# Cosine-weighted attention with a mixture of adapters: narrower moving operands for two kinds of matmul, and a mask applied before the sigmoid

## The chip, the cores and the metric

The kernel runs on one core of one Trainium2 chip. The metric is the device time of one execution in microseconds (us). Three executions of the kernel before took 107.39, 108.11 and 108.67 us; their median is 108.11 us. The profile was taken of one further execution.

A core has five engines with queues of their own: TensorE (PE in the profile; PEld is its weight load), VectorE (DVE), ScalarE (ACT), GpSimd (POOL) and SyncE (SP). All of them feed the same 16 DMA engines.

## The reference, cut to what matters

```python
# q, k, v: (8, 8, 576, 64);  w_gate: (512, 8);  A: (8, 512, 16);  B: (8, 16, 512)
theta = pi / 2 * arange(S) / S
phi(x) = concat([relu(x) * cos(theta), relu(x) * sin(theta)], -1)     # 128 features
q_p, k_p = phi(q), phi(k)
kv  = einsum('bhsf,bhsd->bhfd', k_p, v)
z   = sum(k_p, axis=2)
num = einsum('bhsf,bhfd->bhsd', q_p, kv)
den = einsum('bhsf,bhf->bhs', q_p, z)[..., None] + 1e-6
x   = (num / den), heads side by side: (4608, 512)
...
logits = x @ w_gate
the two largest of 8 logits get softmax weights w, the others none
out = x + sum over the two experts e of  w_e * ((x @ A[e]) @ B[e])
```

For two kept logits the softmax weight of one is a sigmoid of the difference: with s the sum of the two largest, the weight of logit l is sigmoid(2l - s).

## The kernel before, in words

There are eight batches of eight heads with 576 tokens of 64 numbers. The output is made in 36 tiles of 128 rows (two token positions of 64 rows each), numbered n.

Inputs are loaded on POOL's DMA queue (`load_k`, `load_v`, `load_q`, lines 124 to 143), which turns float32 into bfloat16 on the way; only k of batch 0 goes by SP's queue as float32 (`k0f`). There are five buffers each for k, q and v, so batches 5, 6 and 7 reuse buffers of earlier ones; v of batch 5 goes where v of batch 0 was. For batches 1 to 7 the 576 tokens lie on 128 partitions as nine token slots: one half of the partitions has five, the other four (`NJ` = 5, `long_half`). Token slots s = 0 to 3 thus fill 128 partitions, and the fifth, s = 4, only 64 (`half_of`). Batch 0 has another layout with nine slots of 64 partitions.

For each batch and slot, `scale_k1` (line 236) makes the cosine and sine halves of the key features on ScalarE, VectorE or POOL; a relu before POOL's version is `relu_k` on VectorE (line 264). `kv(b, s)` (line 277) then issues eight matmuls, one per head, into two PSUM banks `cd`: the key features are the stationary operand, and the moving operand (`v_rhs`, line 269) is two pieces of 64 columns: v of this head and slot, and 64 columns of ones at the end of the v tile (line 177). So each matmul has 128 columns, of which the first 64 give kv and each of the others gives z. `kv_out` (line 291) copies 65 of them per head.

For each tile n: `transp_q` (Q, line 320) turns q and scales it by a diagonal matrix, `evac_q` (E) applies the relu, `numden` (N, line 364) multiplies by the 65 columns of kv and z, `normalise` (R, lines 375 to 386) divides, `transp_x` and `evac_x` (X and C, lines 394 and 401) turn the result. `logits` (L, line 421) multiplies it by `AW`: 128 columns of all experts' A, then 16 columns of which eight hold the gate weights and eight are zeros (`ZW` = 144). `AW` is filled by two loads (lines 205 and 207) with each expert's columns apart, so the moving operand is nine pieces of 16.

Tiles are gated in groups of three (eleven groups, then one of two tiles and one of one). `gate_a` (A, lines 430 to 438, VectorE) finds the two largest logits, their sum `nm`, the mask of kept logits and `tg` = 2l - nm. `gate_sig` (S, line 447, ScalarE) writes the sigmoid beside the products in PSUM. `gate_b` (B, lines 454 and 456, VectorE) multiplies sigmoid and mask to `em`, and the expert products by `em` to `zg`. Then `transp_z` (Z), `evac_z` (Y), `delta` (O, lines 488 and 489) and `evac_o` (V, lines 502 and 505) follow; for ten tiles `add_x` (P, line 496) adds x on POOL. `store` (T, line 515) writes the 256 KB of a tile by SP's queue.

The order of the work is written out by hand: the words of `ORDER` (lines 31 to 66) are carried out one after the other, under a schedule that keeps each engine to the order in which its instructions are issued. Stores are held back: the load before the last pair (q of batch 7) is followed by a tiny transfer on SP's queue that reads what it brought (`first_loads`, line 562), and every store stands behind that transfer. Before `ORDER`, lines 518 to 544 do the start: tables, 24 warm-up matmuls (line 524), batch 0's keys, and the loads of the next batches and of the weights.

Of the kernel before, what the change touches and what calls it, by code (L numbers as in the profile page):

```python
# [11 lines left out]
ALU = mybir.AluOpType  # L12
# [19 lines left out]
R0 Q1.0 Q1.1 E1.0.a E1.1.d X0 Q2.0 K1.0.0.a K1.2.0.d N1 E2.0.a Q2.1 R1 H E2.1.a Q3.0 C0.a  # L32
K1.4.1.d N2 K1.3.1.d K1.0.1.a Q3.1 R2 H K1.1.0.a X1 H H C1.a K1.2.1.d H E3.0.d E3.1.a M1.2
K1.1.1.a M1.0 K1.3.0.d K1.4.0.d N3 X2 R3 M1.1 M1.3 M1.4 C2.d Q4.0 W1 Q4.1 H E4.0.a E4.1.d H Q5.0
N4 E5.0.a Q5.1 R4 H E5.1.a X3 Q6.0 Q6.1 C3.d E6.0.a H K2.3.1.d N5 E6.1.a U2.0.2 X4 H R5 K2.4.0.a
L0 Q7.0 K2.4.1.a Q7.1 K2.3.0.d N6 G2.0 C4.d E7.0.a L1 R6 L2 E7.1.a X5 Q8.0 C5.a Q8.1 G2.1 A0 N7
E8.0.a X6 R7 M2.4 S0 C6.a Dq.3 M2.3 E8.1.a M2.0 B0 N8 M2.1 U2.2.3 F8 G2.2 L3 R8 L4 L5 Z0 A1 Q9.0
Y0.a Q9.1 Dk.4 M2.2 E9.0.d S1 E9.1.a X7 B1 W2 Q10.0 Q10.1 C7.d E10.0.a N9 O0 X8 R9 E10.1.a Z1 L6
K3.2.0.a L7 O1 U3.0.2 C8.a.1 N10 V0.d G3.0 Q11.0 Q11.1 V1.a R10 L8 E11.0.a O2 E11.1.a G3.1 O3 X9
V2.a V3.d Q12.0 Q12.1 K3.2.1.a A2 N11 Dv.4 M3.0 K3.4.1.d M3.1 S2 K3.3.0.a C9.d M3.2 K3.4.0.d  # L40
E12.0.a R11 X10 Dq.4 M3.4 E12.1.a K3.3.1.a Dk.5 Q13.0 B2 Q13.1 N12 E13.0.a C10.d M3.3 F12
E13.1.a X11 R12 Z2 Dv.5 L9 W3 Q14.0 C11.d.2 Q14.1 N13 E14.0.a O4 U4.0.2 F13 E14.1.a U4.2.3 O5
G4.0 R13 X12 V4.a Q15.0 Q15.1 C12.a V5.d N14 E15.0.a L10 G4.1 K4.4.0.d O6 E15.1.a L11 R14 X13 O7
C13.a Dk.6 Q16.0 V6.d V7.a Q16.1 N15 E16.0.a K4.4.1.d X14 A3 M4.0 F15 E16.1.a G4.2 M4.1 R15 S3
C14.a Q17.0 Q17.1 B3 E17.0.a N16 Dq.5 X15 E17.1.a M4.2 R16 C15.a L12 Dk.7 O8 K4.3.1.a L13 V8.d
L14 N17 K4.3.0.a Z3 A4 Q18.0 F17 Q18.1 Y3.a R17 M4.4 Dq.6 E18.0.a M4.3 S4 E18.1.a U5.0.2 X16 B4
W4 G5.0 Q19.0 Q19.1 C16.d E19.0.a N18 L15 K5.4.1.d E19.1.a X17 R18 O9 G5.1 C17.a Q20.0 Q20.1
E20.0.a L16 V9.d O10 E20.1.a L17 Dv.6 K5.4.0.d N19 V10.d Z4 F19 Q21.0 Y4.a Q21.1 R19 K5.3.1.a
M5.4 M5.1 E21.1.a E21.0.d X18 K5.3.0.a U5.2.3 N20 A5 M5.0 G5.2 F20 C18.a O11 R20 O12 S5 X19
V12.a M5.3 Dq.7 V11.d M5.2 C19.a B5 N21 Dv.7 W5 Q22.0 R21 Q22.1 E22.0.a X20 O13 E22.1.a K6.2.1.d  # L50
Q23.0 C20.a K6.3.1.d N22 U6.0.2 E23.0.a Q23.1 K6.3.0.d G6.0 X21 K6.2.0.d F22 Z5 E23.1.a L18 R22
V13.a Q24.0 Q24.1 E24.0.a C21.d.5 L19 L20 E24.1.a N23 U7.0.2 O14 A6 X22 F23 G7.0 V14.a Q25.0 R23
Q25.1 S6 E25.0.a O15 O16 E25.1.a G6.1 B6 N24 C22.a Q26.0 R24 Q26.1 E26.0.a L21 Z6 P14 X23
E26.1.a L22 U7.2.3 C23.d.6 N25 V15.a Q27.0 V16.a G7.1 R25 Q27.1 X24 K6.4.0.a L23 M6.1 A7 E27.0.a
M6.2 P16 E27.1.a C24.d N26 O17 K6.4.1.a K7.3.0.d M6.0 V17.d M6.3 F26 S7 R26 M6.4 Q28.0 W6 B7
Q28.1 X25 E28.0.a N27 K7.3.1.d O18 C25.d E28.1.a O19 L24 R27 V18.a Z7 T0 X26 Q29.0 P18 C26.a.7
Q29.1 T1 V19.d N28 L25 E29.0.a T2 R28 O20 P15 X27 E29.1.a L26 T3 O21 C27.a Q30.0 V20.d T4 Q30.1
G7.2 V21.a X28 A8 N29 E30.0.a T5 M7.1 R29 E30.1.a M7.0 T6 C28.a O22 M7.3 T7 S8 V22.d K7.4.0.a
N30 X29 T8 B8 K7.4.1.a M7.2 T9 Q31 F30 C29.d M7.4 E31.0.d E31.1.a T10 L27 W7 L28 R30 T11 Z8 L29
Y8.a T12 Q32.0 A9 N31 E32.0.a T13 Q32.1 R31 S9 X30 E32.1.a O23 T14 O24 V23.a Q33 C30.d T15 V24.a  # L60
N32 B9 T16 E33.0.a X31 P24 O25 R32 L30 C31.a T17 O26 E33.1.a V26.d Z9 T18 P21 X32 V25.a N33
# [8 lines left out]
def kernel(ctx, tc, q, k, v, w_gate, A, Bw, out):  # L70
# [7 lines left out]
    ZW = ER + R  # L78
# [17 lines left out]
    VN = H * NJ * D  # L96
# [13 lines left out]
    v_b = [persist.tile([128, VN + D], BF16, name=f"v{b}") for b in range(5)]  # L110
    v_b += v_b[:3]
# [26 lines left out]
    def load_v(b):  # L138
        if b == 0:
            x = v_b[b][:, 0:G * NS * D].rearrange("p (g x) -> p g x", g=G)  # L140
# [35 lines left out]
    for t in v_b[:5]:  # L176
        nc.vector.memset(t[:, VN:], 1.0)
    ones = persist.tile([128, 128], BF16, name="ones")
# [21 lines left out]
    AW = persist.tile([128, E + 1, DCH, R], BF16, name="AW")  # L200
    nc.vector.memset(AW[:, E], 0.0)  # L201
    Ball = persist.tile([128, DM], BF16, name="Ball")

    def load_weights():
        nc.gpsimd.dma_start(out=AW[:, 0:E].rearrange("p e c r -> p e (c r)"),
                            in_=A.rearrange("e (p c) r -> p e (c r)", c=DCH))
# [6 lines left out]
    g_t, u_t, den_t = {}, {}, {}  # L213
# [55 lines left out]
    def v_rhs(b, at, pr):  # L269
        base = v_b[b][pr, at * D:(at + 1) * D]  # L270
        p, (step, n) = base.ap[0], base.ap[-1]
        return bass.AP(base.tensor, base.offset, [p, [(VN - at * D) * step, 2], [step, n]])
# [4 lines left out]
    def kv(b, s):  # L277
        first, last = kv_n[b] == 0, kv_n[b] == kv_all[b] - 1
        kv_n[b] += 1
        for g in range(G):  # L280
            for par in range(2):
                if b == 0:
                    pr = (lo, hi)[par]
                    lhsT, rhs = kp_t[b][pr, s, g], v_rhs(b, g * NS + s, pr)
# [3 lines left out]
                nc.tensor.matmul(out=kvz[par][:, g], lhsT=lhsT, rhs=rhs,  # L288
                                 start=(first and g == 0), stop=(last and g == G - 1))
# [119 lines left out]
    def logits(n):  # L409
        g = group_of[n]  # L410
        i = n - groups[g][0]
        if i == 0:
# [5 lines left out]
            u_t[g] = t[:, 3 * ZW:3 * ZW + 3 * E].rearrange("p (i e) -> p i e", e=E)  # L418
        xT = xT_t.pop(n)
        for c in range(DCH):  # L420
            nc.tensor.matmul(out=za_t[g][:, i, :], lhsT=xT[:, c, :], rhs=AW[:, :, c, :],  # L421
# [3 lines left out]
    def gate_a(g):  # L425
# [3 lines left out]
        for i in range(n):  # L429
# [6 lines left out]
                                in1=m8[:, 0:n, 1].to_broadcast([128, n, 8]), op=ALU.is_ge)  # L436
# [4 lines left out]
        g_t[g] = (t, mask)  # L441

    def gate_sig(g):
        n = len(groups[g])
        t, mask = g_t[g]
        u = u_t.pop(g)
        nc.scalar.activation(u[:, 0:n], t[:, 0:n], AF.Sigmoid)
        g_t[g] = (u, mask)

    def gate_b(g):  # L450
        n = len(groups[g])
        u, mask = g_t[g]
        em = p_g.tile([128, 3, 8], FP32, name="em")
        nc.vector.tensor_tensor(out=em[:, 0:n], in0=u[:, 0:n], in1=mask[:, 0:n], op=ALU.mult)
# [154 lines left out]
```

## Time and profile before

| what | value |
|---|---|
| median of three runs | 108.11 us (107.39 to 108.67) |
| profiled execution, its own time | 107.45 us |
| its span, from first to last instruction | 105.7 us |
| TensorE busy | 94.8 us (90%) |
| VectorE, ScalarE, POOL busy | 87.5, 84.5, 63.1 us |
| POOL's DMA queue (loads) | 13.84 MB, 88.5% of the 16 engines' time |
| SP's DMA queue (first load and stores) | 10.62 MB, 27.0% |

In rows that give groups of instructions, the columns are line, engine, operation, what is written from what is read, shapes and count, then busy time in us and mean ns of one, then idle time before them and what ended it. In rows by time, the first two numbers are the start and the length of a merged run of like instructions, and `x16` is their number. In sums by window there is, behind the window and its length, one busy time for each engine with the number of instructions in brackets, then the granted clock of TensorE, the DMA share and GB/s. Where a window is restricted to one line of the kernel, only the engines that have it are given. In the chain of waits, the numbers are start, length and what the end of the program hung on.

### The profile page before, as it was taken

Reading aid. Unit: us, or ns where it says so; the run is one execution under the profiler, and the core shown is the slowest. Engines: PE = TensorE matmul, PEld = TensorE weight load, DVE = VectorE, ACT = ScalarE, POOL = GpSimd, SP = SyncE. Lnnn points to the kernel's source line nnn. Section 1 sums busy time; section 2 is a strip of 40 time slices with the busy share of each in tenths; the row PEclk is TensorE's granted clock in tenths of the full one; section 3 lists DMA queues with packets and bytes.
Section 4 is the critical chain, followed back from the end, with each engine's and each line's share of the span. In section 5 each row is a group of like instructions: output and inputs, shape, how many; then the busy total and the mean of one; then the engine's idle time right before and its main releaser. Section 6 shows DMA issues by size and latency. Waiting matters only on the chain.

```text
span 105.7 us, 4237 instructions
## 1 busy us (share of the span) xinstructions
PE 94.8 (90%) x1696; PEld 72.6 (69%) x1696; DVE 87.5 (83%) x305; ACT 84.5 (80%) x184; POOL 63.1 (60%) x94
## 2 busy tenths in 40 slices
PE   2999879999999999999899999998999999998700
PEld 1335765876898878877787887867888986775200
DVE  5489469859989989989999999999999998799510
ACT  4359459649975999898999999999699979997800
POOL 5995342254979099899939575699329102984000
PEclk9999999999999999999999999999999999999995
DMA  2999999999999999999999999999799899898991
GB/s 31 372 230 206 200 201 200 204 190 187 205 205 198 202 204 204 193 208 201 198 196 203 206 205 203 198 210 199 99 344 367 333 380 346 325 356 311 385 383 69
DMA packets 26995, 24.72 MB, mean 234 GB/s; under 512 B 2784, under 2 KB 21856, under 8 KB 26976
## 3 DMA queue, kind: packets, MB, share of 16 engines
q0 software_dynamic: 21248, 13.84, 88.5%
q1 hardware_dynamic: 5728, 10.62, 27.0%
q8 instruction: 13, 0.21, 0.7%
q14 instruction: 6, 0.05, 0.1%
HBM read 28.85 MB, written 9.44 MB: 362 GB/s over the span
## 4 chain that ended last, share of the span: by engine, by line
PE 66%; DMA 12%; DVE 11%; ACT 3%; issue 3%; DVEq 0%; ACTq 0%
PE cd L288 15%; PE qd L320 12%; DMA AW<-in_moe_w_gate_dram 12%; PE za L421 8%; PE nd L364 8%; PE wu L524 8%; PE xz L394 7%; PE cd L489 4%; DVE xt L386 3%; PE xz L469 2%; DVE osb L505 2%; PE cd L488 1%; PE dx L489 1%; DVE xT L401 1%; DVE rden L379 1%
## 5 line engine op out<-in xcount | busy, mean ns | idle before, releaser
L336 ACT ACTIVATE qpT<-qd 128x512 bf16<-128x512 f32 x65 | 37.1, 608 | 3.1 <-PE qd L320 2.1
L257 POOL TENSOR_SCALAR kp<-k,tab_kv 128x512 bf16<-128x512 bf16 x32 | 22.0, 697 | 9.5 <-DVE k L267 4.4
L386 DVE TENSOR_TENSOR xt<-nd,rden 128x512 bf16<-128x512 f32 x36 | 24.9, 692 | 2.1
L320 PE MATMUL qd<-diag,q 128*64 128x128 bf16 x544 | 22.8, 223 | 0.1
L288 PE MATMUL cd<-v,kp 128*128 128x128 bf16 (+1 forms) x352 | 21.8, 218 | 0.0
L320 PEld LDWEIGHTS <-q 128*64 128x64 bf16 x544 | 16.7, 110 | 4.6 <-issue 2.0
L288 PEld LDWEIGHTS <-kp 128*128 128x128 bf16 (+1 forms) x352 | 18.2, 96 | 2.2 <-DVE kp L254 0.4
L496 POOL TENSOR_TENSOR osb<-osb,xt 128x512 f32<-128x512 f32 x10 | 11.4, 1159 | 11.1 <-ACT osb L502 11.1
L364 PE MATMUL nd<-kvsb,qpT 128*128 128x65 bf16 (+1 forms) x320 | 15.3, 194 | 1.4 <-DVE xt L386 0.9
L394 PE MATMUL xz<-ident,xt 128*128 128x128 bf16 x144 | 14.1, 221 | 1.3 <-DVE xT L401 0.5
L364 PEld LDWEIGHTS <-qpT 128*128 128x128 bf16 (+1 forms) x320 | 12.1, 100 | 3.4 <-issue 1.0
L421 PE MATMUL za<-AW,xT 128*128 128x144 bf16 x140 | 13.3, 227 | 0.2 <-DMA AW<-in_moe_w_gate_dram 0.2
L394 PEld LDWEIGHTS <-xt 128*128 128x128 bf16 x144 | 10.4, 114 | 3.9 <-DVE xt L386 1.4
L252 ACT ACTIVATE kp<-k,tab_kv 128x512 bf16<-128x512 bf16 (+1 forms) x18 | 12.6, 724 | 0.4 <-DMA k<-in_k_dram 0.3
L502 ACT COPY osb<-cd 128x512 f32<-128x512 f32 x21 | 12.2, 608 | 0.4 <-PE cd L489 0.3
L401 ACT COPY xT<-xz 128x512 bf16<-128x512 bf16 (+1 forms) x19 | 12.3, 648 | 0.2 <-PE xz L394 0.2
L127 POOL DMA_DIRECT2D v<-in_v_dram x14 | 9.7, 701 | 2.7 <-DMA v<-in_v_dram 2.5
L421 PEld LDWEIGHTS <-xT 128*128 128x128 bf16 x144 | 9.7, 98 | 2.3 <-issue 0.7
L127 POOL DMA_DIRECT2D k<-in_k_dram x14 | 9.8, 704 | 2.0 <-DMA k<-in_k_dram 1.4
L524 PE MATMUL wu<-wide,ones 128*128 128x512 bf16 x24 | 8.0, 513 | 2.0 <-DVE AW L201 2.0
L295 ACT CAST kvsb<-cd 128x260 bf16<-128x260 f32 x16 | 5.2, 380 | 4.0 <-PE cd L288 4.0
L136 POOL DMA_DIRECT2D q<-in_q_dram x8 | 6.3, 793 | 3.0 <-DMA q<-in_q_dram 2.6
(80 smaller groups left out, 136.5 us busy)
## 6 DMA issues: line engine op xcount, KB each, us to landing
out_dram<-osb SPq DMA_DIRECT2D x36, 256.0 KB, 3.3
q<-in_q_dram POOLq DMA_DIRECT2D x8, 576.0 KB, 11.0
k<-in_k_dram POOLq DMA_DIRECT2D x7, 320.0 KB, 10.5
v<-in_v_dram POOLq DMA_DIRECT2D x7, 320.0 KB, 11.2
k<-in_k_dram POOLq DMA_DIRECT2D x7, 256.0 KB, 9.7
v<-in_v_dram POOLq DMA_DIRECT2D x7, 256.0 KB, 11.7
k0f<-in_k_dram SPq DMA_DIRECT2D x1, 1152.0 KB, 5.6
v<-in_v_dram POOLq DMA_DIRECT2D x1, 576.0 KB, 7.8
```

Source lines behind the costliest of these rows:

```text
L127: nc.gpsimd.dma_start(out=t[pr, :, 0:n * D], in_=x)
L252: nc.scalar.activation(dst, src, AF.Relu, bias=0.0, scale=tab)
L257: nc.gpsimd.tensor_scalar(out=dst, in0=src, scalar1=tab, scalar2=1.0, op0=ALU.mult, op1=ALU.mult)
L288: nc.tensor.matmul(out=kvz[par][:, g], lhsT=lhsT, rhs=rhs, start=(first and g == 0), stop=(last and g == G - 1))
L320: nc.tensor.matmul(out=t[cols, j, 2 * gi:2 * gi + 2, :], lhsT=q_b[b][:, 2 * gp + gi, s, :], rhs=diag[:, s, i], start=(j == 0 and gi == 0), ...
L336: nc.scalar.activation(t, src, AF.Relu)
L364: nc.tensor.matmul(out=nd[pr, gg, j * W:(j + 1) * W], lhsT=qpT[:, j, pr], rhs=kv_t[b][:, h % 2, h // 2, :], start=(eps_late(n) and j == 0) ...
L386: nc.vector.tensor_tensor(out=x, in0=nd[:, :, :, 0:D], in1=rden.rearrange("p (g j) -> p g j", g=2).to_broadcast([128, 2, 4, D]), op=ALU.mult)
L394: nc.tensor.transpose(out=xz[:, c * 128:(c + 1) * 128], in_=x[:, c], identity=ident)
L401: copy(t[:, 0:c], xz[:, 0:c * 128].rearrange("p (c s) -> p c s", c=c))
L421: nc.tensor.matmul(out=za_t[g][:, i, :], lhsT=xT[:, c, :], rhs=AW[:, :, c, :], start=(c == 0 and i == 0), stop=(c == DCH - 1), skip_group_ ...
L524: nc.tensor.matmul(out=wu, lhsT=ones, rhs=wide, start=True, stop=True)
```

## The change

The fifth token slot of batches 1 to 7 gets a moving operand of 65 columns in one piece: v tiles have, for each head, 16 further columns (`VH` = 5 * 64 + 16) of which the first holds ones, right behind the fifth slot. The other slots keep their two pieces of 64 columns. v of batch 5 moves to the memory of `k0f`. `AW` is laid out with all columns of one chunk side by side, 128 and 8 gate columns (`ZW` = 136); the load of A goes to a tile of its own, `A_sb`, and a VectorE copy (`lay_weights`, word J in `ORDER`) arranges it. The gate's mask is now that of the logits left out; `tm` = -1e30 * mask + tg goes into the sigmoid, which writes `em` to SBUF, and the product of sigmoid and mask goes.

`ORDER` is written anew with many words at other places. Engine by engine the instructions nevertheless keep the order of before: on TensorE nothing changes but column counts, on ScalarE nothing but what the sigmoid reads and writes, on POOL and SP nothing but destinations, and VectorE gets the memsets, the copy J (behind the relu of batch 2's slots 0 and 1, ahead of the normalisation of tile 5) and `tm` at the end of `gate_a` for `em` in `gate_b`. The weights' gate load no longer waits for VectorE (the memset of `AW` is gone).

```diff
-    ZW = ER + R
+    ZW = ER + E
...
-    VN = H * NJ * D
+    VH = NJ * D + 16
+    VN = H * VH
...
-    v_b = [persist.tile([128, VN + D], BF16, name=f"v{b}") for b in range(5)]
-    v_b += v_b[:3]
+    v0n = G * NS * D
+    v_b = [persist.tile([128, v0n + D], BF16, name="v0")]
+    v_b += [persist.tile([128, VN + D], BF16, name=f"v{b}") for b in range(1, 5)]
+    v_b += [k0f.rearrange("p g s d -> p (g s d)").bitcast(BF16)[:, 0:VN + D]] + v_b[1:3]
...
-    for t in v_b[:5]:
+    nc.vector.memset(v_b[0][:, v0n:], 1.0)
+    def ones_v(t):
         nc.vector.memset(t[:, VN:], 1.0)
+        nc.vector.memset(t[:, NJ * D:VN:VH], 1.0)
+    for t in v_b[1:5]:
+        ones_v(t)
...
-    AW = persist.tile([128, E + 1, DCH, R], BF16, name="AW")
-    nc.vector.memset(AW[:, E], 0.0)
+    A_sb = persist.tile([128, E, DCH, R], BF16, name="A_sb")
+    AW = persist.tile([128, DCH, ZW], BF16, name="AW")
...
-        nc.gpsimd.dma_start(out=AW[:, 0:E].rearrange("p e c r -> p e (c r)"),
+        nc.gpsimd.dma_start(out=A_sb.rearrange("p e c r -> p e (c r)"),
                             in_=A.rearrange("e (p c) r -> p e (c r)", c=DCH))
-        nc.gpsimd.dma_start(out=AW[:, E, :, 0:E],
-                            in_=w_gate.rearrange("(p c) e -> p c e", c=DCH))
+        nc.gpsimd.dma_start(out=AW[:, :, ER:ZW], in_=w_gate.rearrange("(p c) e -> p c e", c=DCH))
...
+    def lay_weights():
+        nc.vector.tensor_copy(AW[:, :, 0:ER].rearrange("p c (e r) -> p c e r", e=E),
+                              A_sb.rearrange("p e c r -> p c e r"))
...
                     h, pr = 2 * g + par, half_of(b, s)
-                    lhsT, rhs = kp_t[b][pr, s, h], v_rhs(b, h * NJ + s, pr)
-                nc.tensor.matmul(out=kvz[par][:, g], lhsT=lhsT, rhs=rhs,
-                                 start=(first and g == 0), stop=(last and g == G - 1))
+                    lhsT, at = kp_t[b][pr, s, h], h * VH + s * D
+                    rhs = v_b[b][pr, at:at + W] if s == NJ - 1 else v_rhs(b, at, pr)
+                out = kvz[par][:, g].rearrange("p u d -> p (u d)")
+                nc.tensor.matmul(out=out[:, 0:W] if b and s == NJ - 1 else out, lhsT=lhsT, rhs=rhs,
+                                 start=(first and g == 0), stop=(last and g == G - 1),
+                                 skip_group_check=True)
...
-            nc.tensor.matmul(out=za_t[g][:, i, :], lhsT=xT[:, c, :], rhs=AW[:, :, c, :],
+            nc.tensor.matmul(out=za_t[g][:, i, :], lhsT=xT[:, c, :], rhs=AW[:, c, :],
...
-                                in1=m8[:, 0:n, 1].to_broadcast([128, n, 8]), op=ALU.is_ge)
+                                in1=m8[:, 0:n, 1].to_broadcast([128, n, 8]), op=ALU.is_lt)
...
+        tm = p_g.tile([128, 3, 8], FP32, name="tm")
+        nc.vector.scalar_tensor_tensor(out=tm[:, 0:n], in0=mask[:, 0:n], scalar=-1e30,
+                                       in1=t[:, 0:n], op0=ALU.mult, op1=ALU.add)
...
-        u = u_t.pop(g)
+        g_t[g] = u = p_g.tile([128, 3, 8], FP32, name="em")
         nc.scalar.activation(u[:, 0:n], t[:, 0:n], AF.Sigmoid)
...
-        em = p_g.tile([128, 3, 8], FP32, name="em")
-        nc.vector.tensor_tensor(out=em[:, 0:n], in0=u[:, 0:n], in1=mask[:, 0:n], op=ALU.mult)
...
         for s in range(6, NS):
             make_diag(s)
+        ones_v(v_b[5])
...
+            "W": kv_out, "M": kv, "J": lay_weights,
```

More of the change, by code (lines that the diff above doesn't have):

```diff
@@ L38 @@
[L38 to L49, printed above, removed]
@@ new lines @@
+K4.3.0.a N17 Z3 A4 Q18.0 Dq.6 F17 Q18.1 Y3.a M4.4 R17 E18.0.a M4.3 S4 E18.1.a X16 U5.0.2 Q19.0
+W4 B4 Q19.1 G5.0 N18 E19.0.a C16.d L15 K5.4.1.d E19.1.a X17 R18 O9 C17.a Q20.0 G5.1 Q20.1
+E20.0.a L16 V9.d O10 E20.1.a L17 K5.4.0.d N19 Dv.6 V10.d Z4 F19 Q21.0 Y4.a Q21.1 R19 K5.3.1.a
+M5.4 M5.1 E21.1.a E21.0.d X18 K5.3.0.a U5.2.3 N20 A5 M5.0 G5.2 F20 C18.a O11 O12 R20 S5 X19
+V12.a M5.3 Dq.7 V11.d M5.2 C19.a B5 Dv.7 N21 W5 Q22.0 R21 Q22.1 E22.0.a X20 O13 E22.1.a K6.2.1.d
+Q23.0 K6.3.1.d C20.a N22 U6.0.2 E23.0.a Q23.1 K6.3.0.d G6.0 X21 F22 Z5 E23.1.a K6.2.0.d L18 R22
@@ L66 @@
+V29.a P28 R35 T25 Z10 L34 Y10.a T26 A11 X35 O30 T27 C35.d O31 S11 V30.a B11 L35 T28 V31.a Z11
+A12 O32 Y11.a T29 S12 O33 V32.a B12 T30 Z12 V33.a O34 Y12.d T31 O35 V34.a V35.d T32 T33 T34 T35
 """
@@ L269, in v_rhs @@
     def v_rhs(b, at, pr):
-        base = v_b[b][pr, at * D:(at + 1) * D]
+        base = v_b[b][pr, at:at + D]
         p, (step, n) = base.ap[0], base.ap[-1]
-        return bass.AP(base.tensor, base.offset, [p, [(VN - at * D) * step, 2], [step, n]])
+        return bass.AP(base.tensor, base.offset, [p, [((VN if b else v0n) - at) * step, 2], [step, n]])
     kv_n = {b: 0 for b in range(B)}
```

65 lines of the change are left out of this document (33 added, 32 removed).

## The prediction

> **What bounds the kernel now.** I read the page's slices first, then the sums by window, the chain that ended last, and the rows of the queue that issues the stores.
>
> ```profile
> DMA  2999999999999999999999999999799899898991
> GB/s 31 372 230 206 200 201 200 204 190 187 205 205 198 202 204 204 193 208 201 198 196 203 206 205 203 198 210 199 99 344 367 333 380 346 325 356 311 385 383 69
> ```
>
> The DMA engines are never idle: about 74 us of loads at 200 GB/s (bytes written to SBUF; the float32 read is twice that), then stores at 310 to 385 GB/s.
>
> ```profile
> core 0: us, PE busy (x) PEld busy (x) DVE busy (x) ACT busy (x) POOL busy (x), PEclk, DMA share, GB/s
> 35.00:44.00 9.00, 8.98 (x167) 7.46 (x165) 8.23 (x28) 8.77 (x19) 7.13 (x11) 1.00 1.35 201
> 52.00:68.00 16.00, 16.00 (x314) 13.33 (x312) 15.27 (x49) 15.49 (x36) 10.60 (x16) 1.00 1.34 202
> 68.00:76.00 8.00, 7.27 (x139) 6.11 (x136) 7.66 (x29) 7.48 (x17) 6.31 (x8) 1.00 1.19 184
> ```
>
> In the middle TensorE has no idle time, but ScalarE has 0.23 us of 9.0 and 0.51 of 16, VectorE 0.77 and 0.73: the three are nearly level. From 68 on VectorE makes TensorE wait.
>
> ```profile
> 14.10 12.20 DMA AW<-in_moe_w_gate_dram
> 26.44 0.41 PE za L421 x4
> 31.19 0.24 PE nd L364 x8
> 31.44 0.45 PE cd L288 x8
> 31.89 0.75 PE za L421 x12
> 100.11 0.69 DVE osb L505
> ```
>
> In the chain (start, length, what), nothing computed before 26.3 counts: the gate weights come late in the load queue. Then TensorE carries it to about 87. But what the chain ends in is a store, and stores are their own stream:
>
> ```profile
> 74.49 0.82 SPq L562 DMA_DIRECT2D first_loads<-q  x1
> 75.36 15.17 SPq L515 DMA_DIRECT2D out_dram<-osb  x21
> 89.11 5.62 POOL L496 TENSOR_TENSOR osb<-osb,xt 128x512 f32<-128x512 f32 x5 [6.78 <-ACT osb L502]
> 91.42 3.82 SPq L515 DMA_DIRECT2D out_dram<-osb  x5
> 95.33 6.43 SPq L515 DMA_DIRECT2D out_dram<-osb  x10
> 101.21 0.56 SPq L515 DMA_DIRECT2D out_dram<-osb  x1
> ```
>
> The first store is released by a load (the tiny read of q at 74.49) and goes at 75.36. The queue issues 21 stores until 90.53, is idle until 91.42, then issues 15 with no gap. The last ten start every (101.21 - 95.33)/9 = 0.65 us, which is 262,144 bytes per 0.65 us, 400 GB/s. The one idle stretch is store 21, whose sum is the second of five POOL adds begun at 89.11 (5.62/5 = 1.12 each, so it ends at 91.36). Those adds waited 6.78 us for a ScalarE copy, so they move with the computation. A normal gap between stores is 0.65 - 0.56 = 0.09, so 0.89 - 0.09 = 0.80 us is what computing faster can take out of the stream. The last sum (VectorE, 100.80) is ready 0.41 before its store.
>
> **Fifth tokens.** Seven batches have eight such matmuls each; they go from 128 to 65 columns. Chain rows: eight of 128 columns take 0.45 (56 ns each), eight of 65 columns 0.24 (30 ns). They use 64 rows of the array, the 65-column rows all 128; bounds are a saving of 0 (weight loading takes over) and of 26 ns. Weights for 64 rows show the near end:
>
> ```profile
> 9.97 2.01 PEld L288 LDWEIGHTS <-kp 64*128 64x128 bf16 x72 [0.42 <-issue]
> 26.40:89.00 62.60, 11.32 (x120) 8.01 (x120) 1.00 1.23 229
> ```
>
> 72 of them in 2.01 us is 28 ns, no slower than 30, so I take 26 ns. Batch 1 runs before 26.3, under the weights' load, and gives nothing; six batches, 48 x 26 = 1.25 us.
>
> **Expert products.** 144 to 136 columns. Twelve take 0.75, 62.5 ns each; eight columns of 144 are 3.5 ns. The second row above (line 421 alone) has 120 of them before 89 us: 0.42 us. Bounds 0 and 0.42; the time follows the columns in both shapes above, so 0.42. Together 1.67 us of TensorE before 89.
>
> **Laying the weights.** A new VectorE copy of 512 bf16 per partition, in runs of 16, stands between a relu and a normalisation, and the first expert product needs it.
>
> ```profile
> 12.19 0.88 POOL L205 DMA_DIRECT2D AW<-in_moe_A_dram  x1 [2.16 <-DMA q<-in_q_dram]
> AW<-in_moe_A_dram POOLq DMA_DIRECT2D x1, 128.0 KB, 13.6
> 25.52 0.61 DVE L267 TENSOR_SCALAR k<-k 128x1024 bf16<-128x1024 bf16 x1
> 26.05 0.15 DVE L375 TENSOR_SCALAR den<-nd 128x8 f32<-128x8 f32 x1
> 26.47 0.69 DVE L386 TENSOR_TENSOR xt<-nd,rden 128x512 bf16<-128x512 f32 x1
> 27.35 0.30 PEld L364 LDWEIGHTS <-qpT 128*128 128x128 bf16 x8
> L254 DVE TENSOR_SCALAR kp<-k,tab_kv 128x512 bf16<-128x512 bf16 x12 | 4.1, 353 | 0.0
> L267 DVE TENSOR_SCALAR k<-k 128x512 bf16<-128x512 bf16 x4 | 2.0, 494 | 0.0
> ```
>
> Its input lands at 12.19 + 13.6 = 25.8, before VectorE gets there at 26.05, so it waits for nothing. Bounds: 0.35 us (512 bf16 at the fast rate) and 0.69 (512 at the slow rate of the xt row); I take the 0.49 of the relu, the nearest in that it too reads and writes short runs. VectorE is then 0.49 late: the product at 26.44 starts near 26.6, and the normalised tile, done at 27.16, at 27.65, where the next numerators wanted it at 27.35. TensorE loses 0.3 (0.2 to 0.5). Queued behind the copy are only that normalisation and what follows on VectorE, which has idle time to catch up within some ten us.
>
> **Mask and sigmoid.** Per group, em (after the sigmoid) goes and tm (before it) comes, both on VectorE; the sigmoid writes SBUF instead of PSUM.
>
> ```profile
> L454 DVE TENSOR_TENSOR em<-za,mask 128x24 f32<-128x24 f32 x11 | 1.9, 173 | 0.0
> L438 DVE SCALAR_TENSOR_TENSOR tg<-za,nm 128x24 f32<-128x24 f32 x11 | 2.0, 182 | 0.0
> L379 DVE RECIPROCAL rden<-den 128x8 f32<-128x8 f32 x31 | 6.2, 200 | 1.1 <-ACT den L347 0.3
> L379 DVE RECIPROCAL rden<-nd 128x8 f32<-128x8 f32 x5 | 1.0, 201 | 0.8 <-PE nd L364 0.8
> L447 ACT ACTIVATE za<-tg 128x24 f32<-128x24 f32 x11 | 2.3, 210 | 0.7 <-DVE tg L438 0.6
> ```
>
> tm is of tg's kind: 182 for 173, 13 times, 0.1 us, on VectorE. The path from logits to scaled product keeps its length, since one step moves from behind the sigmoid to before it. Taken as 0; bounds, by the larger of 173 and 182 either way over 13 groups, are ±0.1 in sum and 0.2 in the last group. The reciprocals show that a small VectorE operation takes the same from SBUF (200) as from PSUM (201), so tm gains nothing by its source.
>
> [...]
>
> **Start.**
>
> ```profile
> 0.85 0.41 DVE L177 MEMSET v<- 128x64 bf16 x5
> 9.61 0.52 DVE L254 TENSOR_SCALAR kp<-k0f,sin_tab 128x256 bf16<-128x256 f32 x1
> v<-in_v_dram POOLq DMA_DIRECT2D x7, 320.0 KB, 11.2
> v<-in_v_dram POOLq DMA_DIRECT2D x7, 256.0 KB, 11.7
> ```
>
> Four more memsets of 8 elements, one memset of AW fewer; the two memsets for batch 5 follow the last diag. At worst the 0.41 us of the five now is doubled and the warm-up matmuls start 0.4 later; the landing at 26.3 covers that, as computation waits for it anyway. The load queue on POOL keeps its order; the wait of the gate weights' load on VectorE goes, but the queue ahead of it sets its landing, so nothing. Batch 5's v now goes where k of batch 0 lay, whose last reader ends at 9.61 + 0.52 = 10.1.
>
> **v rows 672 bytes apart instead of 640.** Same packets of 640 and 512 bytes at another pitch. No row has that; bounds below nothing are excluded (no fewer bytes), above I leave open; nearest are k rows of the same sizes, so 0.
>
> **Sum.** TensorE at 89 us: 1.67 - 0.3 = 1.35 earlier. ScalarE and VectorE must follow:
>
> ```profile
> 52.00:68.00 16.00, 3.42 (x36) 2.39 (x36) 1.00 1.34 202
> ```
>
> In 52 to 68 two batches' fifth tokens and these 36 expert products save 0.42 + 0.13 = 0.55 where ScalarE has 0.51, so some 0.2 goes there and in 68 to 76. About 1.1 us are left (0.4 to 1.4). The store stream takes out min(1.1, 0.80) = 0.8. So the span is 105.7 - 0.8 = 104.9 and the execution 107.45 - 0.8 = 106.65. That execution is at the low end of the three runs (107.39 to 108.67), so against their median of 108.11 I predict 107.3.
>
> **Rivals.**
> *The stores are no limit.* The stream also has slow spots (one issue took 1.28 us), and 21 stores in 15.17 are 0.72 each against 0.65 later. If those go when sums come sooner, the whole 1.1 to 1.6 us counts: 106.7. For it: the spots are irregular. Against: the first 21 sums were mostly ready before their stores, so their pace is not the computation's.
>
> ```profile
> 93.96 1.28 SPq L515 DMA_DIRECT2D out_dram<-osb  x1
> ```
>
> [...]
>
> *The other engines eat it.* If the idle 0.23 and 0.51 us of ScalarE are needed gaps, and the copy costs 0.5, little arrives at 89: 0.3 us or so, 107.8. For it: the three engines' level load. Against: the idle time is real in the sums by window.
>
> *Slower: the v rows' pitch slows the loads.* Every store waits for the q load of batch 7, and six batches of v lie ahead of it: 6 x 576 KB at 200 GB/s is 17.7 us. Each per cent slower on v is 0.18 us later for all stores. From 0.8/0.18, 4 to 5%, the gain is gone; at 12% the kernel is 1.3 us slower, 109.4. Against: equal packets.
>
> **Numbers.** Stores' limit 0.50, stores no limit 0.25, eaten 0.13, slower 0.12. The first and third lie within 1% (1.08 us, about what a measurement of this kernel can tell from no change), the second beyond it, the fourth beyond it on the other side: faster 0.25, same 0.63, slower 0.12. The likeliest alone: 106.9 to 107.8. With the bounds of the copy, and the other cases until 2 in 10 are out: 106.5 to 108.4.
>
> **What would show it.** Right: eight fifth-token matmuls in about 0.24 us; expert products at 59 ns; first store still near 75.4; no idle time before store 21, and from there to the end stores every 0.65 with last sums ready more than 0.4 us ahead. Wrong: fifth tokens still at 56 ns; the copy over 0.7 us; a first store at another time than 75; or the idle time still there with sums late.

## The result, and the profile after

The changed kernel takes 108.75 us (median of 20 runs, 108.03 to 109.72), the kernel before 108.33 (20 runs, 107.33 to 108.77): a ratio of 1.0058, 95% interval 1.0033 to 1.0083. I had predicted 107.3 with a range of 106.5 to 108.4, so the time lies outside, on the other side of no change. The profiled execution took 108.17 us with a span of 106.4 (before 107.45 and 105.7).

The groups of the kernel after (busy us, mean ns of one | idle before them):

```profile
L306 PE MATMUL cd<-v,kp 64*128 64x65 bf16 x48 | 2.5, 191 | 0.0
L222 DVE COPY AW<-A_sb 128x512 bf16<-128x512 bf16 x1 | 0.3, 273 | 0.0
L461 DVE SCALAR_TENSOR_TENSOR tm<-mask,tg 128x24 f32<-128x24 f32 x11 | 3.3, 302 | 0.4
L469 ACT ACTIVATE em<-tm 128x24 f32<-128x24 f32 x11 | 2.5, 230 | 3.6 <-DVE tm L461 3.5
```

The surprise is the third row: tm takes 302 ns where I had 182. Next, the stretch from the first expert product to that of the last group (`zb`): sums by window, of before (all engines, line 288 alone, line 421 alone), then of after (all, line 306, line 439).

```profile
26.44:97.26 70.82, 69.22 (x1346) 57.12 (x1347) 65.89 (x224) 64.59 (x144) 48.94 (x65) 1.00 1.19 240
26.44:97.26 70.82, 16.93 (x240) 13.92 (x240) 1.00 1.19 240
26.44:97.26 70.82, 13.32 (x140) 9.47 (x141) 1.00 1.19 240
```

```profile
26.39:98.73 72.34, 68.83 (x1346) 56.14 (x1347) 66.89 (x226) 64.40 (x144) 49.15 (x65) 1.00 1.17 239
26.39:98.73 72.34, 15.70 (x240) 12.99 (x240) 1.00 1.17 239
26.39:98.73 72.34, 12.93 (x140) 9.06 (x141) 1.00 1.17 239
```

Key matmuls fell by 1.23 us and expert products by 0.39: the columns do what I had said of them. Yet TensorE's whole busy time fell by 0.39 only (the ends of matmuls are modelled, so what grew there is not read from it), and the stretch grew by 1.52. An example of what TensorE hung on is the gate of one group on VectorE (start, length), before and after:

```profile
48.98 0.41 DVE L254 TENSOR_SCALAR kp<-k,tab_kv 64x512 bf16<-64x512 bf16 x1
49.41 0.32 DVE L430 MAX8 m<-za 128x8 f32<-128x8 f32 x3
49.76 0.16 DVE L432 TENSOR_REDUCE nm<-m 128x3 f32<-128x6 f32 x1
49.84 0.17 DVE L435 TENSOR_TENSOR mask<-za,m 128x24 f32<-128x24 f32 x1
49.96 0.18 DVE L438 SCALAR_TENSOR_TENSOR tg<-za,nm 128x24 f32<-128x24 f32 x1
50.06 0.19 DVE L379 RECIPROCAL rden<-den 128x8 f32<-128x8 f32 x1
50.35 0.69 DVE L386 TENSOR_TENSOR xt<-nd,rden 128x512 bf16<-128x512 f32 x1
50.96 0.17 DVE L454 TENSOR_TENSOR em<-za,mask 128x24 f32<-128x24 f32 x1
51.17 0.56 DVE L456 TENSOR_TENSOR zg<-za,em 128x384 bf16<-128x384 f32 x1
```

```profile
50.18 0.32 DVE L448 MAX8 m<-za 128x8 f32<-128x8 f32 x3
...
50.73 0.18 DVE L456 SCALAR_TENSOR_TENSOR tg<-za,nm 128x24 f32<-128x24 f32 x1
50.94 0.49 DVE L461 SCALAR_TENSOR_TENSOR tm<-mask,tg 128x24 f32<-128x24 f32 x1
51.36 0.19 DVE L398 RECIPROCAL rden<-den 128x8 f32<-128x8 f32 x1
51.65 0.69 DVE L405 TENSOR_TENSOR xt<-nd,rden 128x512 bf16<-128x512 f32 x1
52.26 0.55 DVE L475 TENSOR_TENSOR zg<-za,em 128x384 bf16<-128x384 f32 x1
```

Read the starts, not the lengths. rden and tg, which don't depend on each other, overlap: rden starts 0.10 us behind tg's start, though tg lasts 0.18. tm, which depends on tg, waits for its end and a little more: it starts 0.21 behind tg's start. So from the first MAX8 to rden it is 0.65 us before and 1.18 after, and xt, for which TensorE waits, comes that much later behind the gate's start. (A normalisation follows the gate in seven of the thirteen groups; in the others it is a copy or a scaling.) Behind xt, em is gone, and zg starts 0.61 after xt's start instead of 0.82.

tm here ends with what GpSimd was doing. Its rows, after:

```profile
49.89 1.51 POOL L271 TENSOR_SCALAR kp<-k,tab_kv 128x512 bf16<-128x512 bf16 x2
51.35 0.81 POOL L140 DMA_DIRECT2D q<-in_q_dram  x1
```

GpSimd's scaling ends at 51.40, tm at 51.43. Four of the thirteen tm are long (0.56, 0.49, 0.39 and 0.59 us), and each ends 0.03 to 0.04 us behind the end of the GpSimd operation that ran when it started; over 0.18 they have 1.3 us together. Two tm that started while GpSimd issued DMAs took 0.18, and so did three that started when a GpSimd operation had only 0.08 to 0.12 us to go.

### The profile page after: what moved, and what is told of

The parts are those of the page before. It is cut to its first block, busy times and chain, and to the rows that moved or that the text cites. A ratio compares the mean times of both kernels' runs of the same rounds, so it can differ in the third digit from the quotient of the medians.

```text
span 106.4 us, 4244 instructions
## 1 busy us (share of the span) xinstructions
PE 94.4 (89%) x1696; PEld 71.5 (67%) x1696; DVE 88.5 (83%) x311; ACT 84.3 (79%) x184; POOL 63.5 (60%) x94
## 4 chain that ended last, share of the span: by engine, by line
PE 58%; DVE 29%; ACT 4%; issue 4%; DVEq 0%; ACTq 0%
PE cd L306 12%; PE qd L339 10%; DVE xt L405 8%; PE nd L383 8%; PE wu L543 8%; PE xz L413 6%; PE za L439 5%; PE cd L508 4%; DVE xT L420 3%; DVE osb L524 2%; DVE rden L398 2%; DVE tm L461 2%; PE xz L488 2%; DVE m L448 2%; DVE qpT L357 2%
## 5 line engine op out<-in xcount | busy, mean ns | idle before, releaser
L306 PEld LDWEIGHTS <-kp 128*128 128x128 bf16 (+1 forms) x352 | 17.1, 96 | 2.1 <-DVE kp L268 0.4
L515 POOL TENSOR_TENSOR osb<-osb,xt 128x512 f32<-128x512 f32 x10 | 11.4, 1158 | 11.3 <-ACT osb L521 11.3
L306 PE MATMUL cd<-v,kp 128*128 128x128 bf16 (+2 forms) x312 | 17.6, 214 | 0.0
L439 PE MATMUL za<-AW,xT 128*128 128x136 bf16 x140 | 12.9, 223 | 0.1
L131 POOL DMA_DIRECT2D v<-in_v_dram x12 | 8.3, 700 | 2.6 <-DMA v<-in_v_dram 2.6
L420 DVE COPY xT<-xz 128x512 bf16<-128x512 bf16 (+1 forms) x17 | 7.7, 450 | 0.0
```

Of the source, the lines that this page charges most:

```text
L131: nc.gpsimd.dma_start(out=t[pr, :, 0:n * D], in_=x)
L306: nc.tensor.matmul(out=out[:, 0:W] if b and s == NJ - 1 else out, lhsT=lhsT, rhs=rhs, start=(first and g == 0), stop=(last and g == G - 1) ...
L420: copy(t[:, 0:c], xz[:, 0:c * 128].rearrange("p (c s) -> p c s", c=c))
```

## The experiments

Theories: *port*: tm has two inputs in SBUF (mask and tg; em had one in PSUM), and such an operation waits for GpSimd, as the ends above suggest (51.43 and 51.40); the name is a label, no run shows what the two engines share. *Place*: whatever its length, tm stands ahead of the sigmoid and of xt, where em stood behind both. The rivals from the prediction are the columns themselves and the loads.

All results first. "Stretch" is as above; "first" is the time from a group's first MAX8 to VectorE's first operation that isn't the gate's, added over 13 groups (in the last group only the gate is left, and it is the time to its second step); "second" is the time from the end of the operation ahead of the gate's second step to zg's start (below zero where zg overlaps it), added. An operation that e5, e8 and e10 move to the sigmoid's place is in neither, but for the last group. All three are from the profiled execution.

| kernel | ratio to before (95%) | stretch | first | second |
|---|---|---|---|---|
| before | 1 | 70.82 | 8.62 | 1.99 |
| after | 1.0058 (1.0033 to 1.0083) | 72.34 | 12.58 | -0.70 |
| e1 tg in PSUM | 1.0031 (1.0006 to 1.0057) | 71.15 | 11.30 | -0.70 |
| e2 columns alone | 0.9974 (0.9942 to 1.0006) | 70.50 | 8.58 | 1.98 |
| e3 mask alone | 1.0101 (1.0063 to 1.0138) | 72.48 | 12.17 | -0.69 |
| e4 before, u in SBUF | 1.0011 (0.9991 to 1.0032) | 71.35 | 8.61 | 2.54 |
| e5 tm late | 1.0381 (1.0335 to 1.0426) | 75.51 | 9.05 | 1.20 |
| e6 dummy in first step | 0.9995 (0.9956 to 1.0033) | 71.09 | 9.63 | 2.00 |
| e7 dummy in second step | 0.9967 (0.9934 to 1.0) | 70.52 | 8.60 | 1.98 |
| e8 mask late | 1.0431 (1.038 to 1.0483) | 76.02 | 8.95 | 3.87 |
| e9 mask behind tg | 1.0012 (0.9984 to 1.0039) | 70.97 | 9.56 | 1.83 |
| e10 mask at the sigmoid | 1.0020 (0.9985 to 1.0055) | 71.49 | 8.70 | 2.96 |
| e11 two dummies, xt only | 1.0031 (1.0001 to 1.0061) | 71.44 | 10.20 | 1.83 |
| e12 before, gate of e9 | 1.0014 (0.9972 to 1.0055) | 71.37 | 9.56 | 1.83 |
| e13 after again | 1.0053 (1.0024 to 1.0083) | | | |
| e14 u in SBUF, columns | 0.9994 (0.9961 to 1.0028) | 71.33 | 9.70 | 1.91 |
| e15 e1 again | 0.9998 (0.9967 to 1.0029) | 71.35 | 11.29 | -0.69 |
| e16 columns alone again | 0.9957 (0.993 to 0.9984) | 70.41 | 8.56 | 1.98 |
| e17 tm in a gap | 1.0003 (0.9976 to 1.0029) | 70.96 | 9.80 | -0.69 |
| e18 columns alone, third | 0.9977 (0.9943 to 1.0011) | 70.94 | 8.59 | 1.99 |

e13 and the kernel after are the same program, so that no second stretch is given. e1 to e4 ran on one chip, so did e5 to e8, e9 to e12, e13 to e16, and e17 with e18.

**Port or place: e1.** tg goes to the free PSUM columns beside the logits.

```diff
-        t = p_g.tile([128, 3, 8], FP32, name="tg")
+        t = u_t.pop(g)
```

> The changed kernel with one edit: tg is written to the free PSUM columns behind the products, so that tm reads only one operand (the mask) from SBUF. Theory (port): tm with two SBUF inputs waits until a running POOL instruction ends; with one it does not. Then all 24-wide tm take about 180 ns (four of eleven took 390 to 595), the four places where TensorE fell behind are gone, and the time is 0.4 to 0.8 us below the kernel before (ratio 0.992 to 0.997). Rival (place): what costs is that the mask now stands ahead of the sigmoid, so ScalarE waits longer for it; then the ratio stays at 1.003 to 1.008, as of the changed kernel. Rival (columns): the copy of the weights, the pitch of v or the 65 columns lose the time; the ratio also stays at 1.003 to 1.008.

```profile
L462 DVE SCALAR_TENSOR_TENSOR tm<-mask,za 128x24 f32<-128x24 f32 x11 | 2.0, 179 | 0.4
```

In the timeline of e1, the same group's tm and the GpSimd row over it:

```profile
51.63 0.18 DVE L462 SCALAR_TENSOR_TENSOR tm<-mask,za 128x24 f32<-128x24 f32 x1
```

```profile
50.57 1.50 POOL L271 TENSOR_SCALAR kp<-k,tab_kv 128x512 bf16<-128x512 bf16 x2
```

With one SBUF input tm starts and ends inside GpSimd's operation: none of the thirteen is long. The port theory holds as to the wait, for 1.3 us of "first"; in time it is 0.0027 here, between runs not made together, and 0.0055 in e13 against e15 on one chip. But e1 is still not faster than before.

**Columns and mask apart: e2 and e3.** e2 is the kernel after with the three gate functions of before:

```diff
-                                in1=m8[:, 0:n, 1].to_broadcast([128, n, 8]), op=ALU.is_lt)
+                                in1=m8[:, 0:n, 1].to_broadcast([128, n, 8]), op=ALU.is_ge)
...
-        tm = p_g.tile([128, 3, 8], FP32, name="tm")
-        nc.vector.scalar_tensor_tensor(out=tm[:, 0:n], in0=mask[:, 0:n], scalar=-1e30,
-                                       in1=t[:, 0:n], op0=ALU.mult, op1=ALU.add)
...
+        em = p_g.tile([128, 3, 8], FP32, name="em")
+        nc.vector.tensor_tensor(out=em[:, 0:n], in0=u[:, 0:n], in1=mask[:, 0:n], op=ALU.mult)
```

e3 is before with the same lines the other way round.

> The changed kernel with the gate of the kernel before (mask multiplied in behind the sigmoid, sigmoid in PSUM): 65 columns, 136 columns and the copy alone. Port and place: 0.992 to 0.997 of the kernel before, since neither a second SBUF input nor the step ahead of the sigmoid is there. Columns: 1.003 to 1.008, as of the changed kernel.

> The kernel before with the changed kernel's gate alone (tm ahead of the sigmoid from two SBUF inputs). Port and place: slower than the changed kernel, which had the narrower matmuls to set against it: 1.008 to 1.020 of the kernel before, with long tm where a POOL instruction runs at its start. Columns: 1.000.

The columns alone are no loss (0.9974, then 0.9957 and 0.9977), which rules out the loads and the copy as the cause; the mask step costs 1% by itself.

**Port without place: e4.** Before, with the sigmoid's output in SBUF, so that em, at its old place, has two SBUF inputs.

```diff
-        u = u_t.pop(g)
+        u = p_g.tile([128, 3, 8], FP32, name="us")
```

> The kernel before with one edit: the sigmoid writes SBUF, so em = sigmoid * mask reads two SBUF inputs, still behind the sigmoid. Port: each em that starts while a POOL computation runs ends when that ends (in the kernel before, two of eleven em start so, at 69.7 and 94.1 us); some em of 250 to 700 ns, ratio 1.001 to 1.006. Place: em as before at 173 ns, ratio 1.000.

```profile
L454 DVE TENSOR_TENSOR em<-us,mask 128x24 f32<-128x24 f32 x11 | 2.5, 226 | 0.0
```

226 ns against 173: two of the thirteen waited for GpSimd (0.27 and 0.65 us), the rest took 0.17. The wait came with the operands and not with tm, and struck four of thirteen in after and two here, by what GpSimd was at.

**Which part of the place: e5 to e8.** e5 is e1 with tm moved into `gate_sig`, behind xt, and e8 is e2 with the mask moved there; both move the lines as they are:

```diff
     def gate_sig(g):
...
+        nc.vector.scalar_tensor_tensor(out=tm[:, 0:n], in0=mask[:, 0:n], scalar=-1e30,
+                                       in1=t[:, 0:n], op0=ALU.mult, op1=ALU.add)
...
     def gate_sig(g):
...
+        nc.vector.tensor_tensor(out=mask[:, 0:n], in0=l,
+                                in1=m8[:, 0:n, 1].to_broadcast([128, n, 8]), op=ALU.is_ge)
```

e6 and e7 are e2 with one needless operation of tm's kind, at the end of `gate_a` or between em and zg:

```diff
+        dm = p_g.tile([128, 3, 8], FP32, name="dm")
+        nc.vector.scalar_tensor_tensor(out=dm[:, 0:n], in0=mask[:, 0:n], scalar=-1e30,
+                                       in1=l, op0=ALU.mult, op1=ALU.add)
```

> The first experiment's kernel (the changed kernel with tg in PSUM, 1.0031 of the time of before), with tm issued at the sigmoid's place in the written order, behind the normalisation xt, in place of the end of the first gate step. If tm costs because it stands ahead of xt, for which TensorE waits (theory xt), the time falls to the ratio of the second experiment, 0.996 to 0.999. If it costs because ScalarE's sigmoid waits for one VectorE operation more (theory sigmoid), tm comes later still and the ratio stays at 1.003 or rises, to 1.008 at most. In the trace, the wait of ScalarE's em for tm, 2.9 us in all before, should grow by some 0.3 to 0.7 us for each of 13 groups under both.

> The second experiment's kernel (the columns alone, with the gate of before: 0.9974 of the time of before), with one VectorE operation more in each group, of tm's size and with one input in PSUM, whose result nothing reads (some 0.18 us, 13 times, 2.3 us of VectorE's time), at the end of the first gate step: ahead of the normalisation xt, and not in the way of the sigmoid. Theory xt: 1.002 to 1.005, as the first experiment. Theory sigmoid: 0.997 to 0.999. If it is only VectorE's load that costs, wherever it stands, this and the next kernel rise by the same.

> The second experiment's kernel with the same needless operation of 0.18 us behind em, at the place where before has its product with the mask: behind xt and behind the sigmoid, ahead of zg. Theories xt and sigmoid: 0.997 to 1.000 (zg comes 0.18 us later, with TensorE's other work to cover it). Load alone: as much above 0.9974 as the kernel with the operation in the first step.

> The second experiment's kernel with the comparison that makes the mask (0.17 us a group, 13 times) taken out of the first gate step and issued at the sigmoid's place, behind the sigmoid's input and behind xt. The number of operations is that of before. If what stands ahead of xt and the sigmoid sets the time (either theory), this gains what the first experiment lost by one operation more there: 0.991 to 0.995. If before has slack there, it stays at 0.996 to 0.999.

e5 and e8 went far beyond every expectation. ScalarE's waits in e5 (us in total, times, longest) show why:

```profile
ACT em L471 <- DVE tm L467: 8.9, 11, 1.5
```

against 4.3, 8 times, in the kernel after. tm then stands behind an xt of 0.69 us and whatever else VectorE has to do, and ScalarE stands still until it has tm, with its copies for TensorE behind the sigmoid. VectorE's gate takes only 0.7 us more in e5 than in e1 (9.05 + 1.20, and 1.03 for the twelve tm that neither counts, are 11.3 us against 10.60), and the kernel is 3.5% slower than e1. e8 is the same by another way: sigmoid and logits share a PSUM tile there, so the sigmoid waited for the mask (9.2 us, 11 times), which I had not thought of.

e7 is the clearest of all. Its rows, and those of before above:

```profile
51.53 0.17 DVE L473 TENSOR_TENSOR em<-za,mask 128x24 f32<-128x24 f32 x1
51.62 0.17 DVE L475 SCALAR_TENSOR_TENSOR dm<-mask,za 128x24 f32<-128x24 f32 x1
51.74 0.56 DVE L478 TENSOR_TENSOR zg<-za,em 128x384 bf16<-128x384 f32 x1
```

zg starts 0.21 us behind em's start with dm between them and without (50.96 and 51.17). The needless operation runs while zg waits for em's result: 13 x 0.17 = 2.2 us of work for nothing (0.9967). The same operation in the first step lengthens that by 0.09 a group (0.9995), though it also held up the sigmoid; the intervals of the two overlap.

**Moving the mask: e9, e10, e12.** u goes to SBUF and the mask to PSUM; the comparison stands behind tg in e9 and e12, and in `gate_sig` in e10. **xt alone: e11** is e2 with two MAX8 on the mask at the end of `gate_a`.

```diff
+        mask = u_t.pop(g)
+        nc.vector.tensor_tensor(out=mask[:, 0:n], in0=l,
+                                in1=m8[:, 0:n, 1].to_broadcast([128, n, 8]), op=ALU.is_ge)
...
-        u = u_t.pop(g)
+        u = p_g.tile([128, 3, 8], FP32, name="u")
...
+        d8 = p_g.tile([128, 3, 8], FP32, name="d8")
+        for i in range(2):
+            nc.vector.max(out=d8[:, i, :], in_=mask[:, 0, :])
```

> The columns alone, with the gate of before (0.9974 of the time of before), but the comparison that makes the mask issued behind tg in place of ahead of it, and so that nothing ties the sigmoid to it: the sigmoid's output u goes to SBUF and the mask to the free PSUM columns beside the logits, where u was. The product em still has one input in each. The sigmoid's input is ready 0.17 us earlier in each group, and xt is not. Theory sigmoid (what stands ahead of ScalarE's sigmoid sets the time): ScalarE's waits for tg fall from 1.4 us to some 0.6, and the ratio to 0.990 to 0.995. Theory xt (what stands ahead of the normalisation sets it): 0.996 to 0.999, as without the move.

> As the kernel with the mask behind tg, but with the mask issued at the sigmoid's place in the written order, so that xt too comes 0.17 us earlier, and the sigmoid does not wait for the mask as it did in the kernel before with this place (1.0431, where u and the logits shared a tile). Theory sigmoid: the same as the mask behind tg, within 0.002. Theory xt: 0.993 to 0.996, and lower than the mask behind tg. If a mask issued so late holds up em, zg and TensorE's transposes, 1.00 or more.

> The columns alone, with the gate of before (0.9974), and two needless MAX8 on the mask (0.16 us each, 0.32 us a group, 4.2 us of VectorE's time in all) at the end of the first gate step: they touch neither the logits' tile nor the sigmoid's, and delay only xt and what follows on VectorE. It is twice the delay of the earlier kernel with one needless operation there (0.9995), whose operation read the logits and so held up the sigmoid too. Theory sigmoid: 0.997 to 1.000. Theory xt: 1.004 to 1.010.

> The kernel before, with 144 columns and fifth tokens as they were, and only the gate of the kernel with the mask behind tg. Against that kernel it tells what the columns are worth where the sigmoid comes earlier. If the columns' gain was eaten by the gate chain, the two differ by some 0.6 to 0.8 % here, and this one is at 0.998 to 1.001. If the columns are off the path that sets the end, the two differ by 0.3 % or less, and this one is at 0.993 to 0.997 under theory sigmoid.

Expected gains of half a per cent did not come, and the table tells why: "first" is 9.56 in e9, longer than the 8.58 of e2. Where the mask stood, between nm and tg, it filled the time in which tg waits for nm (in before nm ends at 49.92 and tg starts at 49.96), so it had cost nothing; behind tg it stands in xt's way. In e10 it is out of xt's way, but "second" grows by a microsecond. The pair e9 and e12 was to tell the columns' worth under another gate; 1.0012 and 1.0014 with their intervals say only that it isn't 0.8%. e11 delays only what follows the gate's first step on VectorE (xt in seven groups), by 0.14 us in a group of three (not the 0.32 I had counted, since the two overlap); the sigmoid waits for tg as long as in e16 (1.3 us, 4 times). It costs some 0.6% against e2, e16 and e18, which ran on other chips: what stands behind the gate's first step is a path by itself.

**The steps side by side: e13 to e16.** e13, e15 and e16 repeat after, e1 and e2; e14 is e2 with two results exchanged.

```diff
-        mask = p_g.tile([128, 3, 8], FP32, name="mask")
+        mask = u_t.pop(g)
...
-        u = u_t.pop(g)
+        u = p_g.tile([128, 3, 8], FP32, name="u")
```

> The changed kernel itself, run beside the three others on one chip so that the parts of its loss can be read against each other: 1.004 to 1.008, as before.

> The columns alone with the gate of before, and only the places of two results exchanged: the sigmoid writes SBUF (some 229 ns) in place of PSUM (211 ns), and the mask goes to the free PSUM columns. The order of all operations and the inputs per operation stay. If the sigmoid's move to SBUF is a part of the mask step's cost, this is 0.002 to 0.004 above the columns alone, as the kernels with the mask behind tg (1.0012 and 1.0014) would suggest. If it is not, both are equal within 0.001, and those two were slow for another reason.

> The first experiment's kernel (the changed kernel with tg in PSUM, so that tm has one input in SBUF) again, on this chip. Theory: 0.002 to 0.004 below the changed kernel (the waits for GpSimd), and 0.004 to 0.007 above the columns alone; above the kernel with the sigmoid's output in SBUF by what the one operation more ahead of the sigmoid and xt costs, 0.002 to 0.004.

> The columns alone (the second experiment's kernel) again, on this chip: 0.995 to 0.999. If 0.9974 was chance and the columns are worth nothing, 0.999 to 1.001.

On one chip: columns alone 0.9957, e15 0.9998, after 1.0053. So the place costs 0.41% here (0.57% in e1 and e2) and the port 0.55% (0.27% from after to e1). Each of these is uncertain by some 0.3%, but the means behind the ratios differ on one chip by more than that in all three pairs (e1 and e2, e15 and e16, e13 and e15). The place also holds the sigmoid's longer write to SBUF (231 ns in the mean in e1, 213 into PSUM in e2). e14 did not isolate the sigmoid's output as it was meant to: its mask is written to the tile from which tg reads the logits, tg waited for it (0.21 us behind the mask's start instead of 0.12), and "first" grew to 9.70.

```profile
49.98 0.18 DVE L454 TENSOR_TENSOR za<-za,m 128x24 f32<-128x24 f32 x1
50.19 0.18 DVE L457 SCALAR_TENSOR_TENSOR tg<-za,nm 128x24 f32<-128x24 f32 x1
```

**tm where it should cost nothing: e17**, beside the columns alone once more (e18). In seven groups tm is issued behind the normalisation's first operation.

```diff
         nc.vector.reciprocal(rden, den)
+        if late_tm:
+            late_tm.pop()()
```

> The first experiment's kernel (tg in PSUM), but in the seven groups whose next VectorE operation belongs to a normalisation (groups 0, 3, 4, 5, 6, 8, 9), tm is issued behind that normalisation's first operation (den or rden), so that VectorE has something independent to do while tg's result comes. Theory (tm costs by its place: as a dependent operation it holds VectorE for some 0.22 us ahead of xt): in these groups the time from the first MAX8 to the normalisation's first operation falls from 0.86 to some 0.64 us, its later operations start no later than without tm, and the ratio comes 0.002 to 0.005 under the same kernel's earlier 0.9998 and 1.0031, to 0.995 to 0.999. If the sigmoid's wait for tm is what costs, it stays at 1.000 to 1.003, since the sigmoid still waits for tm.

> The columns alone with the gate of before, for the third time, beside the kernel with tm in the gap on one chip: 0.995 to 0.998. If the gap version is a better kernel than the columns alone, it is below this one.

```profile
51.23 0.19 DVE L461 SCALAR_TENSOR_TENSOR za<-za,nm 128x24 f32<-128x24 f32 x1
51.33 0.19 DVE L400 RECIPROCAL rden<-den 128x8 f32<-128x8 f32 x1
51.46 0.18 DVE L467 SCALAR_TENSOR_TENSOR tm<-mask,za 128x24 f32<-128x24 f32 x1
51.63 0.69 DVE L409 TENSOR_TENSOR xt<-nd,rden 128x512 bf16<-128x512 f32 x1
```

The mechanism is as expected: xt starts 0.30 us behind rden, as it does without tm, and "first" falls by 1.5 us. The stretch falls by 0.2 to 0.4 against e1 and e15. The ratio, 1.0003, is above the 0.995 to 0.999 that I had expected and no better than e15's; it lies where I had put the case that the sigmoid's wait is what costs, though a gain of 0.2% is below what these runs can tell. The sigmoid's wait for tm stays (2.9 us, 6 times; in e18 for tg 1.6, 5 times), which speaks for that case too, as e11 speaks for xt. How the cost of the place divides between xt and the sigmoid is left open; e11 and e5 show only that each can cost by itself. No version with the new mask is faster than before; the columns alone are the best kernel found, and one of their three intervals (e16) lies below 1.

## Why the prediction was wrong, point by point

**Fifth tokens** and **Expert products** were right: 1.25 and 0.42 predicted (to 89 us), 1.23 and 0.39 measured over the stretch.

**Laying the weights** had the right mechanism: in after the first expert product waited for the copy.

```profile
26.38 0.23 PEld L439 LDWEIGHTS <-xT 128*128 128x128 bf16 x4 [0.45 <-DVE AW L222]
```

The copy took 0.27 us in this trace, but 0.45 in most others that have it (e16 and e18 among them), so my 0.49 was near. That the product started at 26.39, before 26.44, does not show that nothing was lost: the gate weights landed at 25.46 here and at 26.30 in before, and at 25.5 to 26.9 in the other traces. What TensorE lost by the copy no run separates, and the stretch, which begins with that product, leaves it out. **Start** and **v rows 672 bytes apart** were right at nothing: the first store goes at 74.91 (before 75.36), so the loads are not later, and the slower rival falls.

**Mask and sigmoid** is the step that failed: "The path from logits to scaled product keeps its length, since one step moves from behind the sigmoid to before it. Taken as 0". VectorE's part of it is in fact kept: "first" and "second" together are 10.61 us in before and 10.60 in e1. What failed is that a sum is not what the time hangs on. 2.7 us went from behind xt to ahead of xt and of the sigmoid, and on each of these another engine waits: 0.4 to 0.6%. And the price of tm, 182 ns from the row of tg, held only where GpSimd was not in the way: 302 in the mean, 0.3 to 0.55%. No rival of mine let the mask step cost anything; the only slower one was the pitch of v. The profile before held what would have told the place: the starts of em and zg against their lengths. For the port it held only the absence of a row: tg and em each have an input in PSUM, and no VectorE operation there reads two tensors from SBUF, as tm does. I had compared reciprocals, which have one input, and concluded on an operation with two.

The traces show when tm waited: it ended 0.03 us behind GpSimd's scaling (51.43 and 51.40), took 0.18 while GpSimd issued DMAs, and took 0.18 inside GpSimd's scaling once it had one input in PSUM (e1). By what mechanism one engine holds up the other is not shown.

**Sum** failed on both terms. Of the 1.1 us left to TensorE after ScalarE and VectorE, the columns alone show 0.4 us or less (stretches 70.41, 70.50 and 70.94 against 70.82): "The other engines eat it", which I gave 0.13, fits the columns best, though no run separates the engines. The sums by window of e18 show VectorE and ScalarE where they were:

```profile
26.10:97.04 70.94, 67.69 (x1336) 56.16 (x1347) 66.12 (x226) 64.50 (x144) 49.31 (x65) 1.00 1.20 240
```

(65.89 and 64.59 before; ten matmul records are missing here, so TensorE's column isn't comparable.) And the store stream did not give the 0.8 us. The idle time before store 21, which was to go, was still 0.75 us in e2 and 0.88 in e18; and in e16, where its last result was ready 0.7 us sooner than in before (100.08 and 100.80), the stream had no idle time and was longer all the same, 26.93 us for its 36 stores against 26.41, since the stores themselves took longer (the longest 1.97 us, in before 1.28). The stream sets the end there, but its pace is not the constant that I had made of it.

```profile
75.23 26.93 SPq L534 DMA_DIRECT2D out_dram<-osb  x36
```

**What would show it** named idle time in the stream with sums late, and that is what came: in after the queue stood idle for 0.4 to 0.5 us three times among the last ten stores, where before had none behind 91.42. So the computation and not the stream set the end.

```profile
95.87 1.21 SPq L534 DMA_DIRECT2D out_dram<-osb  x2
97.56 1.18 SPq L534 DMA_DIRECT2D out_dram<-osb  x2
99.11 1.17 SPq L534 DMA_DIRECT2D out_dram<-osb  x2
100.68 2.51 SPq L534 DMA_DIRECT2D out_dram<-osb  x4
```

Together: -0.2 to -0.4% for the columns, +0.4 to +0.6% for the place, +0.3 to +0.55% for the port; the sum, +0.3 to +0.95%, holds the measured 0.58%. These parts are differences between the same runs, so that they add up to it proves nothing. The independent test is e3: the mask step alone, on the kernel before, costs 1.0%, and place and port together come to 0.84 (after and e2) and 0.96% (e13 and e16).

## What to carry to other kernels

Price a small VectorE operation by the starts around it, not by its length: in a gap where the next one waited for a result it cost nothing (zg 0.21 us behind em, with dm between them in e7 and without in before), at the end of a dependent chain it cost its length and the handover (0.22 us for an operation of 0.18, e1). When an operation moves within the order of an engine, ask for each place what other engines wait for just behind it; equal work ahead of their input was not equal time ("first" and "second" together 10.60 us in e1 and 10.56 in e2, the ratios 1.0031 and 0.9974). And count the operands in SBUF: with a second one VectorE waited here for a computation that GpSimd was in the middle of, up to 0.4 us (tm in after) and 0.5 us (em in e4).

## What the runs showed of the hardware that was not expected

- In the timelines above VectorE started some operations before the end of one ahead that they don't depend on: rden 0.08 us before tg's end (before), dm 0.08 before em's (e7), tm 0.06 before rden's (e17); but MAX8 0.02 us behind the end of kp (before). One that depended on the operation ahead started 0.03 us behind its end (tm behind tg, after) to 0.10 us (xt behind rden, before).
- A PSUM tile shared by two results is a wait in this program: the mask in the logits' PSUM tile held up tg (e14: 0.21 us behind the mask's start instead of 0.12), and the sigmoid's output in it held up the sigmoid (e8: 9.2 us, 11 times).
- The sigmoid of 24 elements takes 230 ns in the mean into SBUF (after) and 210 into PSUM (before); the medians over all groups are 222 and 194. Its effect on the time was not isolated.
- The copy that lays the weights took 0.27 to 0.29 us in after, e1, e6 and e9 and 0.45 in the twelve other traces that have it. In those twelve GpSimd had begun to issue a DMA 0.3 to 0.6 us before the copy, in the four less than 0.2 us before it, or after its start. Whether that is the cause was not tried.
